# Attention, soft mixture and MLP on one core: a new order for the first four pairs of heads, their loads and their row maxima

## The chip, the cores and the metric

The kernel runs on 1 core of one Trainium2 chip. The metric is the device time of that core in microseconds, the median of several runs. Engines are named TensorE (PE in the rows), VectorE (DVE), ScalarE (ACT), GpSimd (POOL) and SyncE (SP); SPq and ACTq are the transfers that SyncE and ScalarE issue. The profile gives the granted TensorE clock as a share of its upper level, 2.4 GHz; 0.50 is its lower level, 1.2 GHz.

## The reference, cut to what matters

```python
q_rot, k_rot = rotate(q), rotate(k)             # rotary, 4 batches x 8 heads, 576 tokens, 64 wide
scores = scale * q_rot @ k_rot.T
scores = scores - max(scores, axis=-1)
attn = exp(scores); attn /= sum(attn) + 1e-9
attn_out = attn @ v                             # -> x, 2304 tokens x 512
logits = x @ phi                                # 32 slots; softmax over tokens (d) and over slots (c)
slot_out = relu((d.T @ x) @ w1[e]) @ w2[e]      # 8 experts, 4 slots each
y = c @ slot_out
out = silu(y @ w_in) @ w_out                    # 512 -> 2048 -> 512
```

All of it is float32. The edited part is the attention; what comes after it is unchanged.

## The kernel before, in words

The 32 heads are worked two at a time, as 16 pairs. A pair has two halves h (288 queries of both heads) and each half five groups: the remainder key block (c = 4) first and then the blocks 0 to 3, so a pair is ten groups and the attention is groups 0 to 159. In a group `scores` makes TensorE products `st` (line 403 and 404; 392 and 393 for the remainder) and ScalarE's exponential reads them (`e`, line 405; `er`, line 394, is the first one of each half). The products with v (`u`) and the sums come five groups later (`session`).

**The row maxima.** The subtraction of the maximum is a 65th row of the second product: `qb` holds the maxima of the 2 x 576 queries in row 64 and `kb` holds -1. The maxima come from nine units a pair (`max_unit`, `max_reduce`), each 128 queries. With the key differences kd = k[0:288] - k[288:576] (`k_diff`, line 340), TensorE makes q.kd and q.k[288:576], ScalarE takes the relu of the first, VectorE adds the second and reduces to a column of `mx` (line 365). Unit 4 holds the last 64 queries of both heads. When all nine are there, `max_rows` transposes the 128 x 9 columns with TensorE (`psm`), ScalarE copies 9 x 128 to `m`, and a transfer writes them into row 64 of `qb` (`max_copy`; lines 373, 378, 379). For pairs 0 and 15 ScalarE issues that transfer, otherwise SyncE.

**The rotary step.** A pair's q and k, and a copy with the halves swapped, are loaded to `raw` (one transfer of 1152 KB, or pieces for the first pairs), multiplied by the cosine and sine tables `tab` (f0, f1; lines 275 and 278), added (f2, line 281), rounded to a high part by ScalarE (f3, line 285), and the residue is taken by VectorE (f4, line 290). High parts and residues are then moved to other partitions by transfers (`sa`, `kb`, `qb`; m0, m1, m2, and mk, mq, ml for the first two pairs, whose key and query halves are copied separately by f3k and f3q). `raw` has two buffers, p % 2, so the load of pair p waits until pair p - 2 has been moved away.

**The order.** Everything is put into the engines' queues by hand, in program order: each engine runs its own queue in order and waits there for what it needs. `at(g, f)` appends a step to group g, `first(g, f)` puts one in front, and `run(g)` issues them after the group's scores. Offsets such as `ROT_2` are relative to the pair's first group. `MAX_COUNTS` says how many maximum units are issued in each group. Ahead of group 0 stands a straight list: pair 0's and pair 1's rotary steps, nine units of pair 0, its row of maxima and two spells of `warm` products of TensorE. The conversions of later weights (`fetch`, `conv`) and the loads of the experts' weights are placed by group too (`W_IN_AT`, `W_LOADS`, `W_OUT_AT`).

## Time and profile before

| what | value |
|---|---|
| median of 3 runs | 635.74 us (629.95 to 639.93) |
| the profiled execution | 634.98 us, its span 633.2 us |
| TensorE busy in the span | 587.9 us (93%) |
| VectorE, ScalarE, GpSimd busy | 407.0, 359.8, 233.6 us |
| mean granted TensorE clock | 0.975 |

The span is what the trace covers; the rest of the time lies around it. The attention takes some 350 us of it, and its first groups start at 27 us. A share of busy time over the whole span mixes stages; the sections below look at stretches.

### The profile page before, as it was taken

The numbers are of one execution on the slowest core, as the hardware profiler recorded it, in microseconds if no ns is written. First come the engines' busy times: TensorE is split into PE (matmuls) and PEld (weight loads), VectorE is DVE, ScalarE is ACT, GpSimd is POOL, SyncE is SP. The second block draws the span as 40 slices with busy tenths as digits, with TensorE's granted clock in tenths as the row PEclk, the third lists the DMA queues.
The fourth block names the chain that finished last, engine by engine and source line by source line (L and its number), as shares of the span: only waits on it lengthen the run. The fifth ranks groups of instructions, "written<-read, shape, count | busy, mean of one in ns | idle before, by whom it ended". The sixth has DMA issues, their size and how long they took to land.

```text
span 633.2 us, 10521 instructions
## 1 busy us (share of the span) xinstructions
PE 587.9 (93%) x3571; PEld 421.4 (67%) x3571; DVE 407.0 (64%) x865; ACT 359.8 (57%) x920; POOL 233.6 (37%) x195
## 2 busy tenths in 40 slices
PE   5768799999999999999989999799899999999997
PEld 3545467766676766765666434577788888888886
DVE  6687678888798887895643433678755544454452
ACT  3446467776776767775665331588664443444342
POOL 5365548767578566773453000312300000000000
PEclk9678889999999999998999999999999999999999
DMA  6885769977789986878959899734202000020002
GB/s 214 206 216 162 201 145 281 246 217 239 212 231 303 303 245 200 226 237 225 297 199 365 297 389 394 277 122 152 85 1 93 8 0 1 2 100 1 0 1 99
DMA packets 43188, 113.86 MB, mean 180 GB/s; under 512 B 4976, under 2 KB 6272, under 8 KB 41344
## 3 DMA queue, kind: packets, MB, share of 16 engines
q1 hardware_dynamic: 42956, 112.87, 58.3%
q8 instruction: 28, 0.46, 0.3%
q10 hardware_dynamic: 180, 0.34, 0.2%
q14 instruction: 24, 0.20, 0.1%
HBM read 78.12 MB, written 7.60 MB: 135 GB/s over the span
## 4 chain that ended last, share of the span: by engine, by line
PE 70%; ACT 11%; DVE 8%; DMA 7%; issue 3%; SPq 0%; POOL 0%; ACTq 0%; DVEq 0%
PE ops L1186 9%; PE ops L1184 9%; PE ops L1185 9%; PE u L432 8%; PE psmx L351 5%; PE st L403 4%; PE st L404 3%; PE s L441 3%; PE l L926 3%; DMA w_in_raw<-in_w_in_dram 3%; PE hps L1079 2%; PE u L429 2%; PE s L443 2%; PE l L905 2%; ACT e L405 2%
## 5 line engine op out<-in xcount | busy, mean ns | idle before, releaser
L405 ACT ACTIVATE e<-st 128x288 f32<-128x288 f32 x256 | 104.4, 419 | 30.3 <-PE st L404 27.6
L1184 PE MATMUL ops<-wo_hi,ghi 128*128 128x512 f32 x288 | 112.8, 392 | 0.0
L1186 PE MATMUL ops<-wo_hi,glo 128*128 128x512 f32 x288 | 112.4, 390 | 0.0
L1185 PE MATMUL ops<-wo_lo,ghi 128*128 128x512 f32 x288 | 112.4, 390 | 0.0
L1086 DVE TENSOR_TENSOR hps<-hps,g 128x384 f32<-128x384 f32 x96 | 49.8, 561 | 84.4 <-ACT g L1083 84.0
L1083 ACT ACTIVATE g<-hps 128x384 f32<-128x384 f32 x96 | 42.3, 490 | 81.9 <-PE hps L1079 81.6
L403 PE MATMUL st<-sa,sa 128*128 128x288 f32 x256 | 85.9, 337 | 0.2
L365 DVE CUSTOM_DVE_ANT_0 relu<-psmx,relu 128x288 f32<-128x288 f32 x144 | 64.4, 449 | 30.8 <-ACT relu L356 22.6
L417 POOL TENSOR_TENSOR es<-e,e 128x576 f32<-128x576 f32 x31 | 46.5, 1499 | 98.9 <-ACT e L405 98.9
L432 PE MATMUL u<-e,v 128*64 128x288 f32 x512 | 79.9, 430 | 0.0
L404 PE MATMUL st<-qb,kb 65*128 65x288 f32 x256 | 76.2, 299 | 0.0
L403 PEld LDWEIGHTS st<-sa,sa 128*128 128x128 f32 x256 | 49.2, 192 | 23.9 <-issue 14.9
L356 ACT ACTIVATE relu<-psmx 128x288 f32<-128x288 f32 x144 | 60.1, 420 | 8.6 <-PE psmx L351 6.2
L1186 PEld LDWEIGHTS ops<-wo_hi,glo 128*128 128x128 f32 x288 | 54.1, 188 | 11.4
L278 POOL TENSOR_TENSOR raw<-raw,tab 128x576 f32<-128x576 f32 x31 | 54.9, 1776 | 17.4 <-DMA sa<-sa 8.1
L1185 PEld LDWEIGHTS ops<-wo_lo,ghi 128*128 128x128 f32 x288 | 54.1, 188 | 10.0 <-issue 0.4
L1184 PEld LDWEIGHTS ops<-wo_hi,ghi 128*128 128x128 f32 x288 | 54.1, 188 | 9.9 <-issue 0.2
L432 PEld LDWEIGHTS u<-e,v 128*64 128x64 f32 x512 | 36.6, 141 | 31.3 <-issue 16.4
L351 PE MATMUL psmx<-sa,sa 128*128 128x288 f32 x160 | 48.3, 319 | 9.0 <-DVE mx L365 7.4
L422 POOL TENSOR_TENSOR es<-es,e 128x576 f32<-128x576 f32 x31 | 53.8, 1734 | 4.8 <-ACT e L405 3.5
L1092 DVE TENSOR_TENSOR glo<-hps,ghi 128x384 fp32r<-128x384 f32 x96 | 49.4, 551 | 4.9 <-ACT ghi L1089 1.8
L351 PE MATMUL psmx<-kd,sa 128*128 128x288 f32 x160 | 47.4, 313 | 5.2 <-DVE kd L340 4.1
(197 smaller groups left out, 1024.8 us busy)
## 6 DMA issues: line engine op xcount, KB each, us to landing
w<-in_w_dram SPq DMA_DIRECT2D x64, 512.0 KB
sa<-raw SPq DMA_DIRECT2D x56, 288.0 KB
raw<-in_qk_dram SPq DMA_DIRECT2D x13, 1152.0 KB
w_out_raw<-in_w_out_dram SPq DMA_DIRECT2D x16, 512.0 KB
w_in_raw<-in_w_in_dram SPq DMA_DIRECT2D x12, 512.0 KB
v<-in_v_dram SPq DMA_DIRECT2D x15, 320.0 KB
qb<-sa SPq DMA_DIRECT2D x16, 288.0 KB
out_dram<-os SPq DMA_DIRECT2D x18, 256.0 KB
```

Source lines behind the costliest of these rows:

```text
L278: eng.tensor_tensor(out=r[:, hd, 1], in0=r[:, hd, 1], in1=c(1), op=ALU.mult)
L351: pe.matmul(t, lhsT=rem_cols(qa, hd, 128) if u == 4 else qa[:, c0:c0 + 128], rhs=k, start=u != 4 or hd == 0, stop=u != 4 or hd == 1)
L356: act.activation(out=r, in_=t, func=ACTF.Relu)
L365: dve.tensor_tensor_reduce(out=r, in0=mxt.pop((p, u, 1)), in1=r, scale=1.0, scalar=-3.0e38, op0=ALU.add, op1=ALU.max, accum_out=mx[p][:, u ...
L403: pe.matmul(st, lhsT=ka[:, c0:c0 + 128], rhs=qa[:, o:o + HS], start=True, stop=False)
L404: pe.matmul(st, lhsT=kb[0:65, c0:c0 + 128], rhs=qb[0:65, S * hd + HS * h:S * hd + HS * h + HS], start=False, stop=True)
L405: act.activation(out=e[:, hd], in_=st, func=ACTF.Exp, scale=0.125)
L422: add(out=es[p, h], in0=es[p, h], in1=e, op=ALU.add)
L432: pe.matmul(u_ps[p, h][64 * hd:64 * hd + 64, :], lhsT=vt[p][:, c, 64 * hd:64 * hd + 64], rhs=e[:, hd], start=False, stop=c == 3, skip_grou ...
L1184: pe.matmul(t, lhsT=a, rhs=wo_hi[k], start=k == 0, stop=False)
L1185: pe.matmul(t, lhsT=a, rhs=wo_lo[k], start=False, stop=False)
L1186: pe.matmul(t, lhsT=b, rhs=wo_hi[k], start=False, stop=k == 15)
```

## The change

- `raw` gets a third buffer, in the pool `late` (where before only a later weight tile lay): pairs go to buffers by p % 3. The loads of pair 2 start right after pair 0's moves, those of pairs 3 and 4 in groups 3 and 5.
- All of pair 1 and the constants (identity among them) are loaded before pair 0's rotary moves.
- GpSimd copies one word of the first key differences to a token before anything else of pair 1, and so waits until VectorE has written them. VectorE takes pair 0's and pair 1's remaining steps of the start except f1 of pair 1.
- Before group 0 only six of pair 0's nine units are made (0, 1, 2 and 4, 5, 6, those that the first half needs). The other three come in groups 0 and 2, and pair 1's rotary steps, moves, key differences and units in groups -1 to 9 (`START_1`).
- The maxima of pairs 0 and 1 go to row 64 of `qb` without transpose and transfer: TensorE multiplies a column of `mx`, broadcast to 64 columns, with the identity, so that each of the output partitions 64 to 127 holds the 128 maxima as a row, and ScalarE copies partition 64 (`max_direct`). For pairs 2 and 3 the old way stays, but ScalarE issues the transfer.
- The offsets of pairs 2 to 4, the counts of units and the w_in conversions are placed anew; the conversions start at group 19 and end at 129, where they ran from 10 to 120.

```diff
-ROT_2 = (-26, -22, -19, -21, -23, -19, -19, -18, -18, -18, -17, -18, -17)
-ROT_3 = (-31, -25, -27, -26, -26, -24, -23, -23, -22, -16, -22, -19, -15)
-ROT_4 = (-28, -28, -26, -28, -24, -23, -23, -20, -22, -17, -19, -21, -17)
+ROT_2 = (-40, -40, -40, -40, -18, -15, -14, -14, -12, -11, -14, -10, -9)
+ROT_3 = (-26, -20, -25, -22, -24, -20, -20, -17, -17, -16, -17, -16, -16)
+ROT_4 = (-28, -26, -26, -23, -24, -23, -21, -19, -19, -17, -19, -17, -17)
 ROT = (-31, -30, -30, -28, -26, -25, -24, -23, -22, -21, -22, -21, -20)
...
 V_LOAD = -6
-K_DIFF_2 = -14
-K_DIFF_3 = -15
-K_DIFF_4 = -16
+K_DIFF_2 = -9
+K_DIFF_3 = -14
+K_DIFF_4 = -15
 K_DIFF = -17
 QK_LOAD = -35
-QK_LOAD_3 = -54
-QK_LOAD_4 = -31
+QK_LOAD_3 = -27
+QK_LOAD_4 = -35
 MAX_ROW = -5
-MAX_ROW_1 = -4
-MAX_ROW_2 = -4
+MAX_ROW_2 = -3
 MAX_ROW_3 = -5
...
 X_T = ((21, 26), (16, 21), (16, 21), (16, 21))
-W_IN_AT = (10, 20, 30, 40, 49, 60, 70, 81, 89, 100, 110, 120)
+W_IN_AT = (19, 30, 40, 49, 60, 70, 81, 89, 100, 110, 120, 129)
 W_IN_STEPS = (1, 1, 5)
...
 BATCH = (14, 16, 20, 21, 22, 23, 26, 30)
-W_LOADS = (34, 54, 64, 75, 66, 84, 86, 76, 105, 95, 118, 130, 126, 143, 127, 137, 136, 138, 145, 155)
+W_LOADS = (34, 54, 64, 75, 66, 84, 86, 76, 105, 95, 118, 130, 137, 143, 127, 137, 136, 138, 145, 155)
 SCALES = -19
 W_OUT_EARLY = (3, 6, 9, 12)
-W_OUT_AT = ((0, 122, 130, 133), (1, 135, 139, 143))
+W_OUT_AT = ((0, 122, 131, 134), (1, 135, 139, 143))
 EARLY = -10
 MAX_AT = (1, 1, 1, 1, 1, 0, 1, 1, 1, 1)
-MAX_FROM = (6, 2, 6)
-MAX_COUNTS = (0, 1, 2, 2, 2, 2, 0, 0, 1, 1, 1, 1, 1, 2, 2, 0, 1, 1, 1, 1, 1, 1, 1, 1, 1, 2, 1, 1, 1, 1, 1, 1, 1, 1, 2, 1, 1, 1, 1, 1)
+MAX_FROM = 6
+START_1 = (-1, 0, 1, 1, 2, 3, 1, 1, 2, 2, 5, 3, -1, -1, 5, 6, 6, 9)
+MAX_COUNTS = (1, 0, 2, 2, 1, 3, 1, 2, 0, 0, 0, 0, 3, 1, 3, 0, 1, 2, 1, 2, 1, 1, 0, 1, 1, 1)
...
+            token = p1.tile([1, 1], F32, tag="token", name="token")
             raw, vt = {}, {}
...
                 if p not in raw:
-                    raw[p] = rw.tile([128, 2, 2, S], F32, tag=f"raw{p % 2}", name=f"raw{p}")
+                    raw[p] = (rw, rw, late)[p % 3].tile([128, 2, 2, S], F32, tag=f"raw{(1, 0, 2)[p % 3]}", name=f"raw{p}")
                 if heads is None:
...
             load(1, (0,))
-            load(1, (1,), (0,))
+            sp.dma_start(out=cst_sb, in_=cst[:, 0:256])
+            load(1, (1,))
...
+            def max_direct(p, us, wp, tag):
+                t = wp.tile([128, 384], F32, tag=tag, name=f"psr{p}_{us[0]}")
+                for i, u in enumerate(us):
+                    pe.matmul(t[64:128, 128 * i:128 * i + 128], lhsT=mx[p][:, u:u + 1].to_broadcast([128, 64]), rhs=ident, start=True, stop=True, skip_group_check=True)
+                for i, u in enumerate(us):
+                    n = 1
+                    if i and us[i - 1] == u - 1:
+                        continue
+                    while us[i + n:i + n + 1] == (u + n,):
+                        n += 1
+                    act.activation(out=operands(p)[2][64:65, 128 * u:128 * u + 128 * n], in_=t[64:65, 128 * i:128 * i + 128 * n], func=ACTF.Copy)
+
             def max_copy(p):
...
                 act.activation(out=m, in_=mrow.pop(p)[0:9, 0:128], func=ACTF.Copy)
-                (act if p in (0, NPAIR - 1) else sp).dma_start(out=operands(p)[2][64:65].bitcast(F32), in_=m.bitcast(F32))
+                (act if p < 4 or p == NPAIR - 1 else sp).dma_start(out=operands(p)[2][64:65].bitcast(F32), in_=m.bitcast(F32))
...
                 g0 = 10 * p
-                if p >= 1:
+                if p >= 2:
                     at(g0 + Q_COPY, rt(p, 7))
                 if p >= 2:
-                    for o, k, a in ROTARY:
+                    for o, k, a in ROTARY[5 * (p == 2):]:
                         at(g0 + o[min(p, 5) - 2], rt(p, k, *a))
...
                     at(g0 + (QK_LOAD_3, QK_LOAD_4, QK_LOAD)[min(p, 5) - 3], lambda p=p: load(p))
-                if p >= 1:
-                    at(g0 + (MAX_ROW_1, MAX_ROW_2, MAX_ROW_3, MAX_ROW)[min(p, 4) - 1], lambda p=p: max_rows(p), lambda p=p: max_copy(p))
+                if p >= 2:
+                    at(g0 + (MAX_ROW_2, MAX_ROW_3, MAX_ROW)[min(p, 4) - 2], lambda p=p: max_rows(p), lambda p=p: max_copy(p))
                 if p == NPAIR - 1:
...
             def units(p, us):
-                for u in us:
+                for i, u in enumerate(us):
                     for h in range(2):
-                        max_unit(p, u, h, u % 3)
+                        max_unit(p, u, h, i)
                     max_reduce(p, u)
...
             f1(0, dve)
-            f1(1)
             f2(0)
...
             mk(0)
+            f0(1)
             f4(0)
             mq(0)
-            load(1, (1,), (1,))
-            f0(1)
+            f1(1, dve)
             f2(1)
...
             m2()
             ml(0)
             ml(1)
+            pool.tensor_copy(out=token, in_=kds[0][0:1, 0, 0:1].bitcast(F32))
             rot[1] = rotary(1)
             g0, g1, g2, g3, g4 = rot[1][0:5]
             h3k, h3q, nk, nq, nl = rot[1][8:]
             g1(0)
-            sp.dma_start(out=cst_sb, in_=cst[:, 0:256])
             load(2, (0,))
+            load_v(0)
+            load(2, (1,))
+            g1(1)
+            units(0, (0, 1, 2))
+            warm(2)
+            k_diff(0, slice(1, 2))
             g0(0)
-            g1(1)
-            g2(0, pool)
-            units(0, range(3))
-            k_diff(0, slice(1, 2))
+            max_direct(0, (0, 1, 2), ps_st, "st")
+            units(0, (4, 5, 6))
+            max_direct(0, (4, 5, 6), ps_st, "st")
+            g2(0)
             g0(1)
-            g2(1, pool)
-            units(0, range(3, 9))
-            max_rows(0)
-            h3k(0)
-            g3(0, act)
-            nk(0)
-            max_copy(0)
-            h3q(0)
-            load(2, (1,))
-            g4(0)
-            nq(0)
-            h3k(1)
-            g3(1, act)
-            nk(1)
-            h3q(1)
-            g4(1)
-            nq(1)
-            k_diff(1, slice(0, 1))
-            k_diff(1, slice(1, 2))
-            load_v(0)
-            nl(0)
-            nl(1)
-            warm(4)
-            sp.dma_start(out=phi_sb, in_=phi.rearrange("(k p) s -> p k s", p=128))
-            load_v(1)
-            ms = [(1, u) for u in range(9)]
+            g2(1)
+            begin(2)
+            ms = [(0, u) for u in (3, 7, 8)] + [(1, u) for u in (0, 1, 2, 4, 5, 6, 3, 7, 8)]
+            pair_1 = ((lambda: h3k(0), lambda: g3(0, act), lambda: nk(0), lambda: h3q(0)),
+                      (lambda: g4(0), lambda: nq(0)),
+                      (lambda: h3k(1), lambda: g3(1, act), lambda: nk(1), lambda: h3q(1)),
+                      (lambda: g4(1), lambda: nq(1)),
+                      (lambda: k_diff(1, slice(0, 1)),),
+                      (lambda: k_diff(1, slice(1, 2)),),
+                      (lambda: nl(0), lambda: nl(1)),
+                      (rt(1, 7),),
+                      (lambda: load_v(1),),
+                      (lambda: max_direct(0, (3, 7, 8), ps_m, "m"),),
+                      (lambda: sp.dma_start(out=phi_sb, in_=phi.rearrange("(k p) s -> p k s", p=128)),),
+                      (rt(2, 1, 0),), (rt(2, 1, 1),), (rt(2, 0, 0),), (rt(2, 0, 1),),
+                      *((lambda us=us: max_direct(1, us, ps_mx, "mx"),) for us in ((0, 1, 2), (4, 5, 6), (3, 7, 8))))
+            for x, fs in reversed(list(zip(START_1, pair_1))):
+                for f in reversed(fs):
+                    first(x, f)
             for g in range(-35, 0):
                 run(g)
             for g in range(NG + 2):
                 i = g % 10
                 if g < NG:
                     p, h, c = groups[g]
-                    if i == (MAX_FROM[p] if p < 3 else 6) and p + 2 < NPAIR:
+                    if i == MAX_FROM and p + 2 < NPAIR:
                         ms += [(p + 2, u) for u in range(9)]
                     u = [ms.pop(0) for _ in range(min(len(ms), MAX_COUNTS[g] if g < len(MAX_COUNTS) else MAX_AT[g % 10]))]
-                    way = [x[1] % 2 if g < 5 else 0 for x in u]
-                    scores(p, h, c, lambda: [max_unit(*x, 0, y) for x, y in zip(u[0:1], way)])
-                    for x, y in zip(u[0:1], way):
-                        max_unit(*x, 1, y)
+                    scores(p, h, c, lambda: [max_unit(*x, 0) for x in u[0:1]])
+                    for x in u[0:1]:
+                        max_unit(*x, 1)
                         max_reduce(*x)
                     esum(p, h, c)
                 else:
                     u = ()
                 session(g)
-                for x, y in zip(u[1:], way[1:]):
-                    max_unit(*x, 0, y)
-                    max_unit(*x, 1, y)
+                for x in u[1:]:
+                    max_unit(*x, 0)
+                    max_unit(*x, 1)
                     max_reduce(*x)
                 run(g)
```

## Rows read from the trace of the kernel before

**Rows 1.** Stretches: width, busy us of each engine (x instructions), clock, DMA share, GB/s

```profile
13.86:116.65 102.79, 85.22 (x484) 60.22 (x484) 77.50 (x168) 61.08 (x165) 60.77 (x45) 0.87 0.75 201
116.65:270.98 154.33, 148.97 (x1037) 105.91 (x1037) 128.99 (x277) 111.02 (x311) 107.47 (x81) 1.00 0.87 244
341.00:405.00 64.00, 60.14 (x525) 25.91 (x523) 25.40 (x63) 21.61 (x52) 5.64 (x5) 1.00 0.95 352
```

**Rows 2.** Timeline of ScalarE: start, us, engine, line; five first exponentials

```profile
28.27 0.41 ACT L394 ACTIVATE er<-st_r 128x288 f32<-128x288 f32 x1 [1.66 <-PE st_r L393]
...
42.06 0.41 ACT L394 ACTIVATE er<-st_r 128x288 f32<-128x288 f32 x1 [0.79 <-PE st_r L393]
...
78.97 0.42 ACT L394 ACTIVATE er<-st_r 128x288 f32<-128x288 f32 x1
...
116.65 0.46 ACT L394 ACTIVATE er<-st_r 128x288 f32<-128x288 f32 x1
...
270.98 0.46 ACT L394 ACTIVATE er<-st_r 128x288 f32<-128x288 f32 x1
```

**Rows 3.** Stretches of five us within the first pairs

```profile
20.00:25.00 5.00, 4.24 (x14) 2.67 (x14) 4.00 (x13) 2.84 (x7) 0.96 (x1) 0.50 0.54 151
35.00:40.00 5.00, 2.43 (x10) 2.43 (x11) 4.63 (x12) 2.96 (x8) 2.57 (x3) 0.52 0.68 249
```

**Rows 4.** Timeline, 30 to 38 us; in brackets the idle time before and its releaser

```profile
30.19 0.63 DVE L340 TENSOR_TENSOR kd<-sa 128x288 fp32r<-128x288 f32 x1 [3.14 <-DMA sa<-sa]
...
30.75 3.84 DVE L275 TENSOR_TENSOR raw<-raw,tab 128x576 f32<-128x576 f32 x2
...
37.57 0.61 PE L351 MATMUL psmx<-sa,sa 128*128 128x288 f32 x1 [5.57 <-DVE mx L365]
```

**Rows 5.** Timeline, 73 to 79 us: pair 2's row of maxima

```profile
73.00 0.81 SPq L379 DMA_DIRECT2D qb<-m  x1
...
78.06 0.40 PE L393 MATMUL st_r<-qb,kb 65*128 65x288 f32 x1 [2.82 <-DMA qb<-m]
```

**Rows 6.** Timeline, 8 to 14 us

```profile
8.11 0.68 ACT L285 ACTIVATE raw<-raw 128x576 fp32r<-128x576 f32 x1 [6.08 <-DVE raw L281]
...
8.59 3.27 POOL L278 TENSOR_TENSOR raw<-raw,tab 128x576 f32<-128x576 f32 x2 [3.22 <-DMA raw<-in_qk_dram]
...
8.82 1.78 DVE L290 TENSOR_TENSOR raw<-raw 128x576 f32<-128x576 f32 x1 [0.26 <-ACT raw L285]
...
10.53 1.95 DVE L275 TENSOR_TENSOR raw<-raw,tab 128x576 f32<-128x576 f32 x1
...
12.58 0.76 DVE L281 TENSOR_TENSOR raw<-raw 128x576 f32<-128x576 f32 x1
...
13.86 0.46 DVE L340 TENSOR_TENSOR kd<-sa 128x288 fp32r<-128x288 f32 x1
```

**Rows 7.** Groups of instructions, 116.65 to 270.98 us: busy, mean ns, idle before

```profile
L365 DVE CUSTOM_DVE_ANT_0 relu<-psmx,relu 128x288 f32<-128x288 f32 x73 | 32.7, 448 | 6.6 <-ACT relu L356 2.9 <-PE psmx L351 2.9
...
L158 DVE SCALAR_TENSOR_TENSOR w_in<-w_in_raw,w_in 128x512 uint32<-128x512 uint32 x8 | 6.0, 752 | 0.3
...
L480 ACT ACTIVATE x<-xps 128x512 f32<-128x512 f32 x8 | 4.8, 604 | 1.5 <-PE xps L473 1.5
...
L155 DVE TENSOR_SCALAR w_in<-hw 128x512 uint32<-128x512 uint32 x8 | 3.3, 417 | 0.0
```

**Rows 8.** Timeline, 22 to 28 us: pair 0's row of maxima and the first scores

```profile
22.98 0.27 ACT L378 ACTIVATE m<-psm 9x128 fp32r<-9x128 f32 x1 [0.41 <-PE psm L373]
...
23.28 1.31 ACTq L379 DMA_DIRECT2D qb<-m  x1
...
26.91 0.61 PE L392 MATMUL st_r<-sa,sa 128*128 128x288 f32 x1
```

**Rows 9.** Timeline, 92 to 94 us: four transposes

```profile
92.75 0.66 PE L473 MATMUL xps<-cst_sb,xt 128*128 128x128 f32 x4 [0.64 <-ACT x L483]
```

**Rows 10.** The chain in order of time: start, us, what

```profile
200.81 9.62 DMA w_in_raw<-in_w_in_dram
```

## The prediction, made before the changed kernel was run

> **What bounds the kernel now.** I began with the stretches of the whole attention part. From group 40 to group 120 (a group is one key block of one half of one pair, ten groups make a pair) TensorE is busy 148.97 of 154.33 us and VectorE 128.99, so TensorE sets the pace and VectorE stands close behind it at 83.6%. From the first key differences to group 40 the same engines are busy only 85.22 and 77.50 of 102.79 us, at a mean granted clock of 0.87 [rows 1]. So the edited stretch is bound by nothing steadily: it is a chain of waits. The weight stage after the attention has TensorE busy 60.14 of 64 us [rows 1], so what the attention gains is not swallowed there: the later loads are placed by group and move with it.
>
> Next I read the starts of the first exponential of a half pair (ScalarE, once every five groups) [rows 2]. The reader is to take differences: 28.27 to 42.06 is 13.79 us for pair 0's first half, the four halves of pairs 0 and 1 take 50.70 (to 78.97) and those of pairs 2 and 3 take 37.68 (to 116.65). From 116.65 to 270.98 there are 16 halves, 9.65 each. Eight halves at that pace are 77.2 us; they took 88.38. The first eight halves thus hold 11.2 us of excess, beside whatever a sooner start is worth.
>
> Then two places where this excess arises. (a) In 35 to 40 us TensorE is busy 2.43 of 5 us while VectorE is busy 4.63 and the clock falls to 0.52 [rows 3]. The timeline says why: VectorE sits in two rotary products of pair 2 for 3.84 us, and the reduction for which TensorE's next maximum unit waits (5.57 us) is queued behind them [rows 4]. (b) Pair 2's row of maxima is issued by SP at 73.00 and the scores that need it start at 78.06, after a wait of 2.82 us [rows 5]. VectorE's queue, in order, is the scarce thing in (a), a small transfer in (b).
>
> **The change part by part.** The sum is made against the profiled execution: 634.98 us, of which the span is 633.2 and 1.78 lie around it. It is 0.76 below the median of the runs, 635.74.
>
> *GpSimd held.* Of VectorE's passes before the first key differences, the two that coincided with GpSimd's two products (8.59 to 11.86) took 1.78 and 1.95 us; the same kind of pass alone takes 0.76 [rows 6]. With GpSimd waiting, both fall to 0.76 (2.21 us saved) and VectorE takes one product over (0.76 added): the key differences start at 13.86 - 1.45 = 12.4 us. Behind the new wait on GpSimd stand only pair 1's two products, which before started earlier but fed additions much later; VectorE's additions of pair 1 wait for them. Now VectorE also makes those two additions itself (2 x 0.76 = 1.52).
>
> *Loads.* The full load of pair 1 and the 128 KB of constants stand ahead of pair 0's first copy on SP's queue. That is 288 + 128 KB more, some 1.2 us at the 352 GB/s of the weight stage, 2.8 at the 151 of 20 to 25 us [rows 1, 3]. The copy can go out once pair 0's first residue starts (8.82, [rows 6]) and is wanted at 12.4, so I cost it at nothing; without that cover it is 1.2 to 2.8 us. The third buffer frees the loads of pairs 2 to 4 from waiting for copies of pairs 0 to 2. Pair 2's load then stands whole ahead of pair 1's copies on SP's queue; before, pair 1's second key difference waited 3.14 us for such a copy [rows 4]. Bounds: 3.1 gained to 3.1 lost; I take nothing, for the load now leaves some 5 us before the copies are ready.
>
> *Six units, then the scores.* Today nine reductions (0.448 each, [rows 7]) and a transpose stand before the first scores: the transposed rows are copied at 22.98, a ScalarE-issued transfer starts at 23.28, and the scores at 26.91 behind warm-up products [rows 8]. After: from 12.4, the key difference 0.46, one residue 0.76 to 1.95, three reductions 1.35, the second key difference 0.46, one product of pair 1 0.76 to 1.95, three reductions 1.35: the sixth ends at 17.5 to 19.9. Three TensorE products and a ScalarE copy follow: four such 128-column products took 0.66 [rows 9], and the copy lies between 0.27 (9 x 128, [rows 8]) and 0.60 (128 x 512, [rows 7]). ScalarE then has two copies of pair 1 of 0.68 each [rows 6] ahead of the exponential. That gives 20.2 to 22.6. The Trainium skill, page SBUF — State Buffer, section SBUF: two separate sides, calls the ports that VectorE and GpSimd share an exclusive lock, held for a whole instruction while the other is blocked; by that rule GpSimd's two products block the same number of VectorE passes as before, only later, and the end would be the late one. I take 22.0, near the late end, since TensorE's share in 20 to 25 us went at a clock of 0.50 [rows 3] and nothing keeps it warmer now. Against 28.27 the start gains 6.3 us.
>
> *Rows of maxima made by TensorE.* Pairs 0 and 1 lose their transposes and transfers and get nine products (9 x 0.165 = 1.5 us of TensorE, from [rows 9]) and four copies each (some 1.7 us of ScalarE, between the same two ends). TensorE pays 1.5 - 0.3 per pair, 2.4 in all, and loses two warm-up products (their work is nothing but cover). For pairs 2 and 3 the transfer leaves from ScalarE, which was busy 61 of 102.79 us [rows 1]; the issue takes 1.31 of ScalarE [rows 8] instead of 0.81 of SP [rows 5], and it no longer queues behind SP's loads and fetches. The wait (b) goes, I think, wholly; next late there is pair 2's last unit, which now comes at group 17, three groups ahead of its scores.
>
> *New order of pairs 1 to 3.* Pair 1's rotary work moves from before group 0 to groups -1 to 3, and its nine reductions come ahead of most of pair 2's products: the queue of (a) is turned round. But no VectorE work vanishes, it is only moved beside scores. This is why I don't add 6.3 and 11.2. VectorE's own sum decides: 77.50 us of work from the first key differences to group 40, less one weight conversion (the first moves from group 10 to 19; 0.42 + 0.75 us, [rows 7]), plus the two additions 1.52, is 77.9. At the steady share of 83.6% that takes 93.1 us, and group 40 comes at 12.4 + 93.1 = 105.5 instead of 116.65: 11.1 us sooner. TensorE's 85.22 + 2.4 us fit, for many of them ran at half clock.
>
> *The shifted conversions.* One w_in fetch moves from group 5 to 124, its conversion to 129, its write-back to 134; against that one 512 KB weight load leaves group 126 for 137. Bytes near group 125 stay the same, so I put this at nothing; the bound is 9.62 us, the longest fetch on the chain [rows 10]. The w_out conversion that comes a group later costs nothing: its consumer is in the last stage.
>
> Forecast: 634.98 - 11.1 = 623.9 us.
>
> **The rivals.** *Everything overlaps.* If the eight halves run at 9.65 from the new start of 22.0, group 40 comes at 99.2, 17.5 us sooner: 617.5. It asks 77.9 us of VectorE in 86.8, 90%. For it speaks that relief from GpSimd's locking would shrink the 77.9; against it that no long stretch here reaches 90%.
>
> *Only the start is gained.* Pair 1's rotary work, put among pair 0's scores, gives back in groups 0 to 5 what the start gained, or the wait moves to GpSimd: pair 2's second product (group 3) is queued there behind four additions of exponentials, and VectorE's addition at group 5 waits for it with all reductions behind. VectorE's share then ends near 79%, midway between 75.4 and 83.6: 98.6 us, group 40 at 111.0, 5.6 sooner: 629.4.
>
> *The small transfer is no faster.* If pair 2's maxima still land 5.06 us after issue (73.00 to 78.06) from ScalarE, the wait of 2.82 us stays: 626.7. Rows speak both ways: pair 0's, from ScalarE, was issued at 23.28 and kept nobody waiting after 26.91 [rows 5, 8]. The Trainium skill, page DMA: Bandwidth & Descriptors, section Issuing engines are not separate DMA queues, says that transfers started by different engines run on the same 16 engines and interleave, so that another issuer saves its issue time only; by that rule this rival holds, and no row here settles it.
>
> *Slower.* The moved fetch is caught at groups 124 to 129 among the early weight and output loads. ScalarE's queue waits at group 129 for its landing, with the exponentials behind. Were the wait the 9.62 us of the longest fetch plus 2.5 us for a restart at half clock, it would cost 12.1, more than the 11.1 gained: 636.0. It decides from a wait of 11.1 us; the five groups of lead (9.65 us) speak against it.
>
> **How the numbers follow.** Forecast 0.47, all overlaps 0.20, only the start 0.20, the small transfer 0.08, slower 0.05. The likeliest's own range is 620 to 628 (a share of VectorE from 81 to 86%, one point being 1.1 us, and 1 us for the loads). To hold eight in ten the range reaches most of the first two rivals: 616 to 632. A measurement of this kernel can tell about 2% from no change, 12.7 us of 635.74, so 623.0 is the line. The forecast lies just above it and crosses with about 0.4 of its chance, the first rival nearly always, the others almost never: faster 0.40, within 0.56, slower 0.04.
>
> **What would show it.** In the changed profile: the first key difference near 12.4 us; the first exponential near 22; no VectorE pass before it above 0.8 us; no wait of TensorE on a reduction above 2 us in groups 0 to 10; no wait on the row of maxima at group 20; group 40's exponential near 105, and the distance from there to the end unchanged within 1 us. A group 40 at 111 or later would make me wrong by the queue of VectorE, one at 99 by too dear a price for it; a longer way from group 40 to the end would point at the shifted fetch.

## The result and the profile after

The change did not make the kernel faster. Its median is 640.1 us over 18 runs (633.57 to 642.45) against 633.4 over 18 runs of the kernel before beside them (629.51 to 639.93): a ratio of 1.0103, 95% interval 1.0077 to 1.0130. The profiled execution took 639.35 us, with a span of 637.2 where that of before has 633.2. The forecast of 623.9 was wrong in its sign, and the time lies outside the range. Of the 15.5 us between it and the profiled execution 11.9 lie before group 40 (117.41 instead of 105.5, below), 3.2 behind it, and 0.4 outside the span.

The first exponentials of the half pairs (as [rows 2], ScalarE's timeline) show where the time went:

```profile
21.77 0.41 ACT L408 ACTIVATE er<-st_r 128x288 f32<-128x288 f32 x1
31.51 0.41 ACT L408 ACTIVATE er<-st_r 128x288 f32<-128x288 f32 x1
...
61.10 0.41 ACT L408 ACTIVATE er<-st_r 128x288 f32<-128x288 f32 x1 [0.34 <-PE st_r L407]
75.76 0.41 ACT L408 ACTIVATE er<-st_r 128x288 f32<-128x288 f32 x1 [0.39 <-PE st_r L407]
...
117.41 0.46 ACT L408 ACTIVATE er<-st_r 128x288 f32<-128x288 f32 x1
```

Take the differences to the kernel before. The scores start 6.50 us sooner (21.77, was 28.27), and at group 5 the lead is 10.55 (31.51, was 42.06). Then it melts: 3.21 us are left at group 20 (75.76, was 78.97), and at group 40 the changed kernel is 0.76 late (117.41, was 116.65). From group 40 to 120 it takes 153.83 us (154.33 before), from there to the last half pair's first exponential at group 155 71.26 (70.25), from that one to the end 294.70 (291.97). In a sum: -6.50 + 7.26 - 0.50 + 1.01 + 2.73 = 4.0 us, the difference of the spans. So there are two losses to explain: the lead lost between groups 5 and 40, and 2.7 us in a stage that the diff doesn't touch.

The stretches, with columns as in [rows 1] (first key differences to group 40, group 40 to 120, ten us around group 12, and the first ten us of the weight stage):

```profile
12.84:117.41 104.57, 88.90 (x514) 62.67 (x514) 75.98 (x168) 61.99 (x168) 58.62 (x45) 0.90 0.68 192
117.41:271.24 153.83, 148.66 (x1037) 105.65 (x1037) 128.94 (x277) 111.20 (x312) 107.12 (x81) 1.00 0.87 244
45.00:50.00 5.00, 1.58 (x12) 0.91 (x8) 3.89 (x4) 1.02 (x3) 2.04 (x2) 1.00 0.99 231
50.00:55.00 5.00, 4.55 (x21) 2.53 (x22) 0.47 (x2) 1.32 (x3) 2.98 (x3) 0.66 0.39 80
362.00:372.00 10.00, 8.44 (x64) 3.40 (x67) 1.56 (x9) 0.00 (x0) 0.00 (x0) 0.83 0.88 324
```

VectorE's work in the edited stretch came out near its cost (75.98 us; 77.9 in the sum), but it fills 72.7% of the stretch, not 83.6. TensorE stood idle for 15.67 us of it (104.57 - 88.90), where it was 17.57 before (102.79 - 85.22, [rows 1]): the waits changed their places more than their sum. TensorE does 1.58 us of work in 45 to 50 us, and then works at a mean granted clock of 0.66, between its levels of 1.2 and 2.4 GHz. The waits of TensorE up to group 40 (us in total, times, longest) say what it waited for (`psmx` is a product of a maximum unit, `psm` the transposed maxima, `rs` the factors of the normalization):

```profile
PE psmx L353 <- DMA sa<-raw: 3.9, 1, 3.9
PE psmx L353 <- DVE kd L342: 3.0, 3, 1.1
PE psmx L353 <- ACT relu L358: 2.4, 5, 1.4
PE psm L375 <- DVE rs L469: 1.8, 1, 1.8
PE psm L375 <- DVE mx L367: 1.2, 1, 1.2
```

The waits on a reduction of [rows 4] are gone from the head of this list. Before, it began so:

```profile
PE psmx L351 <- DVE mx L365: 7.4, 2, 5.6
PE psmx L351 <- DVE kd L340: 4.1, 2, 2.7
PE st_r L393 <- DMA qb<-m: 3.2, 2, 2.8
```

Others have come in their place. The timeline shows the two longest, and the one in the weight stage:

```profile
42.75 3.54 SPq L296 DMA_DIRECT2D sa<-raw  x4
46.34 1.38 SPq L296 DMA_DIRECT2D kb<-raw  x1
48.25 0.75 DVE L342 TENSOR_TENSOR kd<-sa 128x576 fp32r<-128x576 f32 x1
50.45 0.41 PE L353 MATMUL psmx<-kd,sa 128*128 128x288 f32 x1 [3.87 <-DMA sa<-raw]
51.73 0.46 DVE L367 CUSTOM_DVE_ANT_0 relu<-psmx,relu 128x288 f32<-128x288 f32 x1 [2.73 <-PE psmx L353]
...
70.43 0.27 PE L375 MATMUL psm<-cst_sb,mx 128*9 128x128 f32 x1 [1.83 <-DVE rs L469]
71.03 1.33 ACTq L393 DMA_DIRECT2D qb<-m  x1
74.80 0.44 PE L407 MATMUL st_r<-qb,kb 65*128 65x288 f32 x1
...
364.40 4.91 PE L916 MATMUL l<-w,si 128*32 128x512 f32 x28 [1.56 <-DVE lt L890]
```

First, pair 2's moves into `sa` and `kb`, which the new order puts at groups 9 and 11, leave SP between 42.75 and 47.7. The first maximum unit of pair 2 (group 12) needs those into `sa` and starts at 50.45, 7.7 us after the first issue; VectorE's reduction waits behind it. Second, the transpose of pair 2's maxima now stands at group 17 instead of 16; the single bank it is written to holds the sums of pair 1's first half, and it waits until VectorE has read them for the normalization. Third, the first expert product waits 1.56 us for VectorE to copy the last transposes. Before, it waited for nothing:

```profile
361.49 2.78 PE L905 MATMUL l<-w,si 128*32 128x512 f32 x24
```

The compiled programs give the reason: up to the last transposes both kernels take 312 tiles from the three score banks (the output buffers of TensorE that scores, warm-up products and the last transposes take in turn), but the new start takes and frees them in another order, and from there on the turn is another one. The last transposes come to lie in bank 0, where the first expert product wants to write, instead of bank 1.

### The profile page after: what moved, and what is told of

The parts are those of the page before. It is cut to its first block, busy times and chain, and to the rows that moved or that the text cites. A ratio compares the mean times of both kernels' runs of the same rounds, so it can differ in the third digit from the quotient of the medians.

```text
span 637.2 us, 10542 instructions
## 1 busy us (share of the span) xinstructions
PE 592.0 (93%) x3601; PEld 424.4 (67%) x3601; DVE 404.0 (63%) x868; ACT 362.4 (57%) x926; POOL 228.4 (36%) x193
## 5 line engine op out<-in xcount | busy, mean ns | idle before, releaser
L446 PE MATMUL u<-e,v 128*64 128x288 f32 x512 | 78.4, 424 | 0.0
L280 POOL TENSOR_TENSOR raw<-raw,tab 128x576 f32<-128x576 f32 x30 | 53.4, 1782 | 12.1 <-DMA raw<-in_qk_dram 7.5
L1100 ACT ACTIVATE ghi<-hps 128x384 fp32r<-128x384 f32 x96 | 45.5, 492 | 10.1 <-DVE hps L1097 10.1
```

Of the source, the lines that this page charges most:

```text
L280: eng.tensor_tensor(out=r[:, hd, 1], in0=r[:, hd, 1], in1=c(1), op=ALU.mult)
L446: pe.matmul(u_ps[p, h][64 * hd:64 * hd + 64, :], lhsT=vt[p][:, c, 64 * hd:64 * hd + 64], rhs=e[:, hd], start=False, stop=c == 3, skip_grou ...
```

## The experiments

My theory after reading this: the start is worth what was booked, and it is lost to particular waits that the new order creates (moves that land late, a bank held by the sums, the rotation of banks), not to a sum of VectorE's work. The rivals: VectorE's sum or a stretched start sets the pace after all; or the loss lies in the parts that the prediction called gains (the issuer of the row, the hold of GpSimd). Each verdict is a ratio to the kernel before, with a 95% interval.

**The bank in the weight stage.** The changed kernel, with one more score bank drawn in the warm-up and no other instruction changed:

```
-            warm(2)
+            warm(1)
+            warm(1)
```

> The changed kernel with its two warm-up products ahead of the first row of maxima in two tiles instead of one: the same work, but the score banks then rotate so that the last transposes of the attention no longer lie in the bank that the first expert product writes. Theory (the bank costs the 1.56 us wait at 364 us, and the slower clock after it): from the last half pair's first exponential to the end 2 to 3 us less than the changed kernel's 294.7, the groups before it the same within 1 us, ratio about 1.006. Rival (the wait is for a late weight, not for the bank): no difference, ratio 1.010.

Measured: 1.0012 (0.9984 to 1.0039), down from 1.0103, and more than the 1.006 that the theory gave. The wait at the first expert product is gone, the way from group 155 to the end is 292.45 us (294.70), and group 40 comes at 116.73 (117.41). Then the same shift put into the kernel before, where it moves the last transposes from bank 1 into bank 0:

```
-            warm(4)
+            warm(2)
+            warm(2)
```

> The kernel before with its four warm-up products in two tiles of two: the same work, but the score banks turn so that the attention's last transposes lie in the bank of the first expert product. Theory (the bank, not the change's own steps, costs the time after the attention): 2 to 3 us more after the last half pair's first exponential (294 to 295 us instead of 292.0), ratio 1.003 to 1.005. Rival (a late weight or chance): no difference.

Measured: 1.0092 (1.0059 to 1.0125): this alone costs the kernel before as much as the whole change did. In its timeline the wait stands at the same product:

```profile
364.80 3.83 PE L906 MATMUL l<-w,si 128*32 128x512 f32 x20 [1.56 <-DVE lt L880]
```

The way from group 155 to the end is 296.5 us instead of 291.97. The wait is a third of that. Most of the rest is TensorE itself: its same 1585 products keep it busy for 282.49 us, not 279.70, at a mean clock of 0.97 in the 130 us behind the wait (1.00 before). One half pair, from group 40, also took 13.72 us there, with ScalarE waiting 4.11 us for a landing of w_in (1.92 before); I see no tie of that to the bank, and leave it open. A last one tells the shared bank from any shift at all: three parts of warm-up, so that the last transposes lie in bank 2.

```
-            warm(4)
+            warm(2)
+            warm(1)
+            warm(1)
```

> The kernel before with its warm-up split in three, so that the last transposes lie in score bank 2 (before: 1; the split in two put them in bank 0, where the first expert product lies, and cost 0.9%). Theory (it is the shared bank): no wait of the first expert product, the stretch from the last exponential to the end 291.5 to 293 us, time within 0.4% of the kernel before. Rival (splitting the warm-up, or any shift of the banks, costs): 1.006 to 1.012 again.

Measured: 1.0010 (0.9985 to 1.0036), no wait at the first expert product, 291.7 us from group 155 to the end. So it is the shared bank. All the profiles agree: in the seven kernels whose last transposes lie in bank 0, the wait is 1.56 us and the way to the end takes 294.7 to 296.5 us; in the other seven there is no such wait, and it takes 291.0 to 292.5. That is 3.4 us or 0.5% in the mean. The 0.9% of the two ratios is more than this stage explains, and what the rest is isn't shown.

**Pair 2's moves.** In the changed kernel, the two steps that feed the moves and the moves themselves come one to four groups sooner (rotary steps relative to group 20):

```
-ROT_2 = (-40, -40, -40, -40, -18, -15, -14, -14, -12, -11, -14, -10, -9)
+ROT_2 = (-40, -40, -40, -40, -18, -15, -14, -14, -14, -12, -14, -14, -12)
```

> The changed kernel with the last steps of pair 2's rotation sooner: high part and residue of the second head in group 6 instead of 8 and 10, moves in group 8 instead of 9 and 11. Theory (TensorE stood 3.9 us in group 12 for these moves, and then ran at the lower clock): the first half of pair 1 takes 13 to 14.5 us instead of 17.1, group 40 comes 2 to 4 us sooner than 117.4, ratio 1.004 to 1.007. Rival (VectorE's queue is the limit and the landing only hid it): the wait moves to the key differences or a reduction, the half stays at 16.5 or more, ratio 1.010.

Measured: 1.0031 (0.9993 to 1.0070). The half from group 10 takes 14.22 us (17.09 in the changed kernel) and group 40 comes at 115.32, as the theory had it, but TensorE still waits at group 12, now 2.6 us for the key difference. That stands in VectorE's queue behind an addition that waits for GpSimd's product:

```profile
48.22 0.76 DVE L283 TENSOR_TENSOR raw<-raw 128x576 f32<-128x576 f32 x1 [2.66 <-POOL raw L280]
48.90 0.75 DVE L342 TENSOR_TENSOR kd<-sa 128x576 fp32r<-128x576 f32 x1
```

This is the mechanism of my second rival (VectorE's addition behind GpSimd's additions of exponentials), seven groups later than I had put it. The distance to the end was 295.5 us here, so the bank was still paid.

**The wait filled instead of removed.** Warm-up products in the hole at group 12; their banks also move the last transposes to bank 1, so the run is compared with the first one.

```
                 session(g)
+                if g == 11:
+                    warm(7)
```

> The changed kernel with seven idle warm-up products at the end of group 11, where TensorE stands 3.9 us for pair 2's moves; this also turns the score banks away from the first expert product. Theory (half of what a wait costs is the lower clock in the stretch behind it): the wait is filled, the granted clock of 50 to 55 us stays at 1.00 instead of 0.66, the first half of pair 1 takes 1 to 2 us less than 17.1, and with the banks the ratio is 0.998 to 1.001. Rival (the clock behind the wait hides under VectorE's work): the half keeps its 17 us, and only the banks' 2.5 us are gained, 1.001 to 1.003.

Measured: 0.9990 (0.9958 to 1.0022). The clock of 50 to 55 us stayed at 1.00, and the half from group 10 takes 15.60 us instead of 17.09, both as the theory had it. But the one from group 0 took 11.84 (9.74), and beside 1.0012 the difference is within the intervals: a gain in the whole time is not shown.

**The transposed maxima.** They take a bank of the maximum units' pool, for pair 2 alone:

```
-    t = ps_m.tile([128, 512], F32, tag="m", name=f"psm{p}")
+    t = ps_mx.tile(..., tag="mx", ...) if p == 2 else ps_m.tile(..., tag="m", ...)
```

> The changed kernel with the transposed maxima of pair 2 in a bank of the maximum units instead of the single bank that the sums of group 17 hold until VectorE has normalised. Theory (that bank made TensorE wait 1.83 us in group 17, and the slower clock behind it cost about as much again): the second half of pair 1 takes 11.5 to 13 us instead of 14.7, ratio 1.005 to 1.008. Rival (the transpose really waits for the last reduction of pair 2): the wait stays above 1.5 us, ratio 1.010.

Measured: 1.0061 (1.0040 to 1.0082). The wait of 1.8 us is gone, the half from group 15 takes 12.92 us (14.66) and the next 8.74 (10.01).

**The three together, and the key difference sooner.** The first run has the edits of the bank, the moves and the transposed maxima. The second adds one line, so that the key difference no longer stands behind the addition that waits for GpSimd:

```
-K_DIFF_2 = -9
+K_DIFF_2 = -10
```

> The three edits together: score banks turned, pair 2's moves sooner, its row of maxima in another bank. Theory (three separate costs): they add, group 40 at 110 to 113 and the tail 2 to 3 us shorter, 632 to 635 us, ratio 0.995 to 1.000. Rival (one resource behind all, VectorE): less than half of the sum, ratio above 1.004.

> The three edits, and pair 2's key differences at the head of group 10 instead of group 11, that is ahead of pair 3's rotary steps in VectorE's queue, where VectorE stood 2.66 us for a GpSimd product. Theory (what is left of that half is VectorE waiting for GpSimd in order): the first half of pair 1 takes 11 to 12.5 us instead of 14.2, ratio 0.992 to 0.995. Rival (VectorE is short of time): the time comes back within the next halves, ratio 0.997.

Measured: 0.9975 (0.9944 to 1.0006) and 0.9929 (0.9895 to 0.9964). The last is the lowest ratio of the study and the only one whose interval lies below 1 (medians 631.1 us and, beside it, 634.7). But its interval overlaps the one without the line, so what the line is worth isn't shown. Its half from group 10 takes 12.76 us (14.20 without the line; 11 to 12.5 expected), and by group 40 that is lost again, as the rival said. The exponentials of group 40, without the line and with it:

```profile
113.18 0.46 ACT L408 ACTIVATE er<-st_r 128x288 f32<-128x288 f32 x1
```

```profile
113.71 0.46 ACT L408 ACTIVATE er<-st_r 128x288 f32<-128x288 f32 x1
```

What stays in the edited stretch of the second:

```profile
12.80:113.71 100.91, 86.09 (x514) 61.13 (x514) 75.83 (x168) 61.73 (x168) 59.07 (x45) 0.93 0.71 199
```

VectorE is at 75.1% and TensorE at 85.3%, and no wait of TensorE is longer than 1.6 us. One more step in the same direction, pair 3's transposed maxima in the other pool and a group later (-4 where it was -5):

```
+MAX_ROW_P3 = -4
-    ... if p == 2 else ...
+    ... if p in (2, 3) else ...
```

> As the run before, and pair 3's maxima transposed one group later, in a bank of the units, since TensorE stood in group 25 for the last reduction of pair 3. Theory: the second half of pair 2, 15.4 us in the run with three edits, takes 12 to 14 us, group 40 at 106 to 110 us, ratio 0.987 to 0.993. Rival (that half is held by pair 4's key differences and by the additions of exponentials): it stays at 15, ratio as in the run before.

Measured: 0.9969 (0.9934 to 1.0004), not to be told from the run before (its median is 630.8 us). The half took 15.13 us, and group 40 came at 114.18: the rival held. A key difference now kept TensorE waiting 2.3 us.

**VectorE's sum.** Ten passes that nobody reads, added to the changed kernel in the edited stretch and in the steady one:

```
+for g in (12, 16, 20, 24, 28, 62, 66, 70, 74, 78):
+    at(g, lambda: dve.tensor_tensor(out=extra, in0=tab[:, 0], in1=tab[:, 1], op=ALU.add))
```

> The changed kernel with ten added VectorE passes of 576 columns (a sum of the two tables into a tile that nobody reads), five at groups 12 to 28 and five at groups 62 to 78, some 1.2 us each, 6 us in each stretch. The prediction's step (VectorE's sum at a ceiling of 83.6% sets the pace): from the exponential of group 60 to that of group 90 it takes 58.35 + 7 = 65 us. Rival (TensorE, 96% busy there, sets the pace, and VectorE has 9 to 10 us of room): 58.35 to 60 us there. For groups 10 to 35 (64.55 us): by the room alone (21 us idle) nothing to 1 us; if what counts is where VectorE's passes stand in line rather than their sum, 2 to 6 us.

Measured: 1.0295 (1.0219 to 1.0372). The stretches from group 10 to 35 and from 60 to 90, with the passes:

```profile
44.19:116.39 72.20, 57.43 (x303) 38.98 (x302) 49.92 (x99) 35.32 (x97) 35.02 (x27) 0.81 0.59 156
164.37:225.90 61.53, 56.73 (x394) 39.56 (x394) 52.12 (x105) 42.30 (x118) 40.87 (x32) 1.00 0.89 250
```

and without them, in the changed kernel:

```profile
44.01:108.56 64.55, 53.99 (x303) 37.22 (x302) 43.27 (x94) 35.11 (x96) 33.87 (x27) 0.87 0.66 175
155.86:214.21 58.35, 56.15 (x394) 39.75 (x394) 47.83 (x100) 42.07 (x117) 41.01 (x31) 1.00 0.92 261
```

In the steady stretch VectorE goes from 82 to 84.7% and the time grows by 3.18 us, for 4.29 us more of VectorE's busy time; I had put 7 for a ceiling and at most 1.65 for room, and it lies between. TensorE's waits on reductions grew from 0.8 to 3.2 us there. The edited stretch is the lesson: VectorE had been idle for 21 of 64.55 us, and 6.65 us more of busy time cost 7.65 us, with the clock down from 0.87 to 0.81. I had put 2 to 6 us there: even this was too low. Idle time was no room, since the passes stood ahead of reductions and of the normalization that TensorE waits for (3.1 us longest for a `psm<-mx`, 1.2 in the changed kernel).

**The row's issuer.** The changed kernel with the rows of pairs 2 and 3 on SP's queue again:

```
-    (act if p < 4 or p == NPAIR - 1 else sp).dma_start(out=operands(p)[2][64:65]...)
+    (act if p == NPAIR - 1 else sp).dma_start(out=operands(p)[2][64:65]...)
```

> The changed kernel with one part undone: the rows of maxima of pairs 2 and 3 leave from SP's queue again instead of ScalarE's. Theory (the part was worth what the prediction booked, 2.8 us at group 20): TensorE waits 2 to 3 us on the moved row just before the scores of group 20, the half of groups 15 to 20 takes 16.5 to 17.5 us instead of 14.66, and the time stands at 1.010 to 1.016 of the kernel before. Rival (who issues makes no difference, or the slot was idle anyway): no such wait over 0.5 us, that half stays within 0.7 us of 14.66, and the ratio stays at 1.010.

Measured: 1.0040 (0.9998 to 1.0083), no dearer than the changed kernel. The theory failed; the rival was right that the issuer doesn't tell in the time, though not in its numbers (the half takes 12.66 us, and the wait is over 0.5). The row leaves at 69.66 and its scores wait 1.09 us, not 2 to 3 (the releaser shown is a load, whose tile this product doesn't read).

```profile
69.66 0.89 SPq L393 DMA_DIRECT2D qb<-m  x1
...
73.28 0.37 PE L407 MATMUL st_r<-qb,kb 65*128 65x288 f32 x1 [1.09 <-DMA raw<-in_qk_dram]
```

But an issue by ScalarE doesn't keep the wait away either. In the run with the key difference sooner, ScalarE issues the same row, and TensorE waits longer:

```profile
64.42 1.33 ACTq L393 DMA_DIRECT2D qb<-m  x1
...
70.13 0.58 PE L407 MATMUL st_r<-qb,kb 65*128 65x288 f32 x1 [1.58 <-DMA qb<-m]
```

What differs is the traffic. From the issue of the row to its scores the DMA engines were busy for a share of 0.84 in the kernel before (wait 2.82), 0.68 and 0.67 in these two (1.09 and 1.58), and 0.12 in the changed kernel (none). So I read the wait (b) as gone because the new order issues the row with few transfers around it; no run changes the traffic alone. These rows agree with the rule of the Trainium skill that the prediction cited (DMA: Bandwidth & Descriptors, Issuing engines are not separate DMA queues): transfers interleave on the same 16 engines, whoever starts them.

**The hold of GpSimd.** The changed kernel without the copy that holds it:

```
-            pool.tensor_copy(out=token, in_=kds[0][0:1, 0, 0:1].bitcast(F32))
```

> The changed kernel without the one GpSimd copy that holds GpSimd until the first key differences. Theory (GpSimd's passes stretch VectorE's beside them): GpSimd starts its passes of pair 1 before 12 us, one or two of VectorE's four passes of 0.75 us become 1.6 to 1.9 us, the first key differences start 1 to 2 us later than 12.84, and the first exponential 0.5 to 2 us later than 21.77. Rival (the order alone made the start short): GpSimd's pass finds its loads not landed or the passes stay at 0.75 us, key differences stay within 0.3 us of 12.84 and the first exponential within 0.5 us of 21.77 or earlier. In either case the whole time stays within 0.5% of that of the changed kernel (1.010 of the kernel before), since the lead is lost by group 40 anyway.

Measured: 1.0093 (1.0063 to 1.0124), first key differences at 12.84 as with the hold, first exponential at 22.03 (21.77). GpSimd's product starts when its load has landed, and stretches one pass, but the key difference, which with the hold waits for its move until 12.84, starts no later:

```profile
9.69 0.75 DVE L279 TENSOR_TENSOR raw<-raw,tab 128x576 f32<-128x576 f32 x1
9.91 1.79 POOL L279 TENSOR_TENSOR raw<-raw,tab 128x576 f32<-128x576 f32 x1 [4.54 <-DMA raw<-in_qk_dram]
10.48 1.84 DVE L282 TENSOR_TENSOR raw<-raw 128x576 f32<-128x576 f32 x1
...
12.84 1.55 DVE L341 TENSOR_TENSOR kd<-sa 128x288 fp32r<-128x288 f32 x1
```

That key difference takes 1.55 us, not 0.46, but the second one takes 0.45 (1.74 with the hold). VectorE's pass that starts at 10.48 ends 0.62 us after GpSimd's product (11.70). The exclusive lock of the Trainium skill (SBUF — State Buffer, SBUF: two separate sides), by which a VectorE instruction with two SBUF inputs and a GpSimd one that reads SBUF block each other, the later one until the first is over, agrees with this.

## Why the prediction was wrong

**The start: right, by 0.2 us.** The changed kernel's timeline, beside [rows 6], and the stretch of 20 to 25 us, beside [rows 3]:

```profile
8.56 0.76 DVE L277 TENSOR_TENSOR raw<-raw,tab 128x576 f32<-128x576 f32 x1
9.23 0.75 DVE L292 TENSOR_TENSOR raw<-raw 128x576 f32<-128x576 f32 x1
9.90 0.75 DVE L280 TENSOR_TENSOR raw<-raw,tab 128x576 f32<-128x576 f32 x1
10.69 0.76 DVE L283 TENSOR_TENSOR raw<-raw 128x576 f32<-128x576 f32 x1
...
12.84 0.46 DVE L342 TENSOR_TENSOR kd<-sa 128x288 fp32r<-128x288 f32 x1 [0.90 <-DMA sa<-sa]
13.36 0.65 POOL L809 COPY token<-kd 1x1 f32<-1x1 f32 x1 [7.99 <-DVE kd L342]
14.05 2.76 POOL L280 TENSOR_TENSOR raw<-raw,tab 128x576 f32<-128x576 f32 x2
...
15.39 1.74 DVE L342 TENSOR_TENSOR kd<-sa 128x288 fp32r<-128x288 f32 x1
```

```profile
20.00:25.00 5.00, 2.98 (x17) 2.13 (x16) 4.70 (x9) 4.89 (x12) 1.08 (x1) 1.00 0.71 264
```

No pass before the key differences is above 0.76. They start 0.44 later than 12.4, since the copy that I had costed at nothing behind the loads arrives 0.90 late. The sixth unit ends at 19.31 (17.5 to 19.9), the first exponential comes at 21.77 (22.0). But the closeness is in part luck. The credit for the hold of GpSimd was misplaced: without it the exponential moved by 0.26 us. The terms of the sum add to 19.7 to 22.4, not 20.2 to 22.6, and 22.0 was taken for a clock of 0.50 in 20 to 25 us, which was 1.00. What is left to make the start short is that six units, and no transposed row with its transfer, stand ahead of the scores; no run undoes that alone.

**From the start to group 40: the step that failed.** It reads "VectorE's own sum decides: 77.50 us of work from the first key differences to group 40", taken "at the steady share of 83.6%". The sum was right within 2 us (75.98), and the share did not carry over. In the steady stretch TensorE is 96% busy, and I read 83.6% as what VectorE needs at that pace (the passes added there cost 3.18 us, between a ceiling's price and none, so this reading is not settled); in the edited stretch of before, VectorE stood at 75.4% for the waits of a chain, and the new order made another chain at 72.7%, with 15.67 us of waits of TensorE for 17.57. I removed the waits that I saw and asked of none of the new places (group 9 for the moves, 17 for the transposed maxima, 11 for the key difference) whether its inputs would have landed, or its bank be free, by then. The changed constants gave those groups. With the moves and the transposed maxima put elsewhere, and the bank of the weight stage freed, 1.0103 became 0.9975; with the added passes in the edited stretch VectorE's share moved from 67 to 69% while the time grew. The account is not complete: in the runs with three and with four edits group 40 still comes at 113.2 and 113.7 us, some 8 us behind the forecast's 105.5, and no run tells what holds it there. I can't split the lost 11 us between groups 5 and 40 among the causes to a tenth: the edits' gains (0.9, 0.7, 0.4%) add to more than the 1.3% of the three together, and the intervals are 0.4 to 0.8% wide.

A smaller term was too low: the rows of maxima of pairs 0 and 1 were put at 2 x 1.5 us of TensorE, and the trace has 6.2 us in 36 instructions for their 18 products.

```profile
L381 PE MATMUL psr<-cst_sb,mx 128*64 128x128 f32 x36 | 6.2, 302 | 1.1 <-DVE mx L367 1.1
```

**The row of pair 2.** The wait (b) went wholly in the changed kernel, as forecast, but not for the reason given, the issuer: with ScalarE issuing too the row reached its scores 5.71 us after its issue in the run with the key difference sooner, with 1.58 us of waiting. So the third rival was wrong on this kernel's time and right on the mechanism.

**The weight stage.** "The distance from there to the end unchanged within 1 us" failed: 519.79 instead of 516.55 us. I named the shifted fetch as what would be to blame, and it is not: the waits of ScalarE for w_in come to 3.1 us against 3.0 from group 40 on, and the three bank experiments show the shared bank, worth 2.3 us (undone in the changed kernel) to 2.7 (the stage's loss) of the 3.2 in the profiles. The prediction has no term for it. That the start takes its tiles from the rotating score banks in another order could be read from the diff (a product of maxima now stands between units that share the pool). Where the turn would then stop was the price to ask for.

**The rivals.** "Only the start is gained" came nearest in its mechanism, and its queue behind GpSimd was there, at group 12 instead of 5; but the lead of its 5.6 us was lost too. The slower rival had the right sign and the wrong place.

## What to carry to other kernels

The busy share of an engine in a steady stage is no measure of how fast it will go in a stage bound by waits: for a new order, go through each moved step and ask when its inputs land and when its buffer or bank is free, and count the waits it makes against those it removes. Follow also the turn of each rotating pool past the edit, since a shift by one can put a late reader into the bank that another stage writes first, hundreds of us away. An idle engine has room only if what is queued behind the added work has time to wait.

## What was not expected of the hardware

The granted clock after the same waits is not the same in each execution. In the changed kernel and in the one with the row on SP's queue, which differ only from group 17 on, TensorE's waits from 44 to 62 us were the same (3.9 us at group 12 the longest), and the half from group 15 then went:

```profile
61.10:75.76 14.66, 12.34 (x61) 8.30 (x60) 8.89 (x23) 6.73 (x20) 7.00 (x6) 0.73 0.70 201
```

```profile
61.30:73.96 12.66, 9.14 (x61) 6.29 (x60) 9.03 (x23) 6.74 (x20) 6.94 (x6) 1.00 0.82 232
```

The 61 instructions of TensorE took 12.34 us at a mean clock of 0.73 and 9.14 at 1.00 (all at 2.4 GHz), and the half 2 us less, for which I see no cause in TensorE's work. Two executions of one and the same kernel, the one with the moves sooner, took 632.38 us at a mean clock of 0.989 and 640.58 at 0.973. A single profile of such a kernel is thus no measure of a wait of one or two us, and the medians of ten runs, with intervals of 2.7 us and more, barely are.

Of the ten added VectorE passes of 576 columns, the four that started with no GpSimd instruction under way took 0.74 or 0.75 us, one that met only the end of such an instruction 0.92, and the other five 1.65 to 1.97 (8.3 us for the five of the edited stretch, 5.1 for those of the steady one), while a reduction out of the maximum units' bank stayed at 0.45 beside GpSimd's products at 14 to 16 us. What a pass costs is decided by where it is put.
